# LayerNorm row statistics on ScalarE, the maxima fold on one operand, and a new table of orders

## The chip, the core and the metric

The kernel runs on one core of a Trainium2 chip. The metric is the device time of one execution in microseconds (us). The core's engines are TensorE (PE in the profile, its weight loads PEld), VectorE (DVE), ScalarE (ACT) and GpSimd (POOL); SyncE (SP) issues nearly all DMAs. Each engine works through its own instruction stream strictly in order and waits on semaphores for the others.

## The reference

Four attention layers act on x of 1 x 2048 x 512, in the order A, B, A, B; both kinds have 32 heads of 16 dimensions.

```python
x = x + _A_ref(_layernorm(x), A_wqkv, A_wo)   # 8 keys per query, 2 apart
x = x + _B_ref(_layernorm(x), B_wqkv, B_wo)   # sliding window of 256 keys
x = x + _A_ref(_layernorm(x), A_wqkv, A_wo)
x = x + _B_ref(_layernorm(x), B_wqkv, B_wo)

def _layernorm(x, axis=-1, eps=1e-5):
    m = jnp.mean(x, axis=axis, keepdims=True)
    v = jnp.var(x, axis=axis, keepdims=True)
    return (x - m) / jnp.sqrt(v + eps)
```

## The kernel before

The 2048 rows are cut into 8 chunks of 256 rows (`C`), and a layer works chunk by chunk; layers 0 and 2 are of kind A, 1 and 3 of kind B. In names such as `xn0_5_1` the digits are the layer, the chunk and the half (128 rows) of the chunk.

**Norm.** `norm(l, c)` handles one chunk: for each half, VectorE's `bn_stats` and `bn_aggr` (L750, L751) give mean and variance in `mv`; GpSimd turns them into scale and shift in `rs` (`rstd`, L754 to L757); ScalarE writes the normalised rows `xn` (L769) and their 16-bit rounding `xm` (L781); GpSimd or VectorE writes the remainder over `xn` (L772); and four transposing DMAs on SyncE's queue bring both into `xh` and `xl` (L775, L778). `xn` has two buffers, one for each half, so a chunk's `xn` may be written only when the remainder of the norm before has left by DMA.

**Layer A.** Projections `pq` (L802 to L804; three 16-bit matmuls for each product), copied to `q` and `kv` by ScalarE; products `pr` of query and shifted keys and their sums (L960, L967, on VectorE or GpSimd); a reduction on TensorE into `L`; the softmax over 8 keys in `e`; spread on TensorE (`pb`), weighted values `pw` (L1046) and their sums `o`.

**Layer B.** `eh` and `el` (16-bit parts of the projections) go through DRAM (`re`) into the stacked operands `stk`. TensorE forms scores twice. The first time (`st`, `sf`, L1130) is for the maximum over each query's keys: VectorE masks (L1153) and reduces them (L1154, L1173) into the tile `m`, which holds for each row one maximum from `st` and one from `sf`. `mturn` takes the larger of the two (L1183) and transposes the result (L1184); ScalarE and GpSimd split it into two 16-bit parts `mt` (L1187 to L1191), and it goes through DRAM (`md`) into spare rows of `stk`. The second time (`sk_F`, `sk_L`, `sk_H`, L1224) the matmul thereby subtracts the maximum; ScalarE takes the exponential `p` (L1234), GpSimd masks it (L1245), TensorE multiplies with the values (`av`, L1259).

Both kinds end in `finish`: `oh` and `ol`, output projection `po` (L823), and `done` (L869), in which VectorE adds `po` to the rows of x in `xr`. The norm of layer B works on those rows.

**The order.** Every step is a task with an engine, a duration, and what it reads and writes. The table `ORDER` gives each task its place in its engine's stream; a negative number puts the task on its other engine (`alt`: VectorE in place of GpSimd or the reverse). `Plan.order()` plays the streams against the durations, which sets only in what sequence the engines' instructions are written out and which buffer a tile gets; within an engine the table decides. In the scope `W`, 80 groups of three matmuls on constants (`idle`) fill TensorE while the weights are prepared.

Of the kernel before, what the change touches and what calls it, by code (L numbers as in the profile page):

```python
# [1415 lines left out]
```

## Time and profile before

| | |
|---|---|
| time, median of 3 runs | 1371.41 us (1362.38 to 1377.51) |
| the profiled execution's own time | 1373.37 us |
| its span, first to last instruction | 1371.6 us |
| mean granted TensorE clock | 0.973 |
| PE busy | 1246.9 us, 91% of the span |
| DVE busy | 1142.3 us, 83% |
| POOL busy | 955.4 us, 70% |
| ACT busy | 733.7 us, 53% |
| DMA | 140.17 MB, mean 102 GB/s |

The busy time of an engine is that of its instructions; an engine that waits for another is idle. A row of groups gives the source line, the engine, the operation, its tiles (written <- read), the count, the busy time, the mean of one, and the idle time before these instructions with what ended it. A row of waits reads "engine, instruction <- what it waited for: us in total, times, longest".

### The profile page before, as it was taken

To read this page: it belongs to the slowest core of one execution; us is meant where nothing else is said; L and a number is where in the kernel's file an instruction comes from. 1 tells how busy PE (TensorE), PEld (TensorE's weight loads), DVE (VectorE), ACT (ScalarE), POOL (GpSimd) and SP (SyncE) were. 2 spreads that over 40 slices of the span, in tenths; PEclk is the share of its full clock that TensorE was granted. 3 is DMA by queue.
4 is the path that set the end of the run, shared out by engine and by line. 5 is a ranking of instruction groups with operands and counts; after the bars stand their busy time and mean duration, and the time that the engine had idled before them with its cause. 6 is when DMAs were issued, how large, how long until landed. Compare 5 with 4: busy or idle time off the path is not lost.

```text
span 1371.6 us, 47863 instructions
## 1 busy us (share of the span) xinstructions
PE 1246.9 (91%) x20752; PEld 847.8 (62%) x20752; DVE 1142.3 (83%) x1482; ACT 733.7 (53%) x1035; POOL 955.4 (70%) x1013
## 2 busy tenths in 40 slices
PE   6869999989998898999999999998998999998877
PEld 4546666657566665666667666766666666664544
DVE  5968978887887888789899999798987988988574
ACT  7543454646555464655556464555555566365544
POOL 4357678778686877877686768888678877666233
PEclk9989999999999999999999999999999999999989
DMA  8204243334434332444434444433444434234322
GB/s 279 60 16 137 60 126 90 121 84 121 82 78 129 94 112 69 115 110 106 119 90 124 106 115 108 99 108 78 136 100 111 93 97 118 54 96 112 97 73 64
DMA packets 172467, 140.17 MB, mean 102 GB/s; under 512 B 105184, under 2 KB 131296, under 8 KB 172256
## 3 DMA queue, kind: packets, MB, share of 16 engines
q1 hardware_dynamic: 172000, 136.85, 38.1%
q8 instruction: 162, 2.65, 0.8%
q14 instruction: 49, 0.40, 0.1%
q10 hardware_dynamic: 256, 0.26, 0.1%
HBM read 67.11 MB, written 43.48 MB: 81 GB/s over the span
## 4 chain that ended last, share of the span: by engine, by line
PE 20%; DVE 12%; DMA 7%; SPq 4%; issue 3%; ACT 2%; POOL 2%; ACTq 0%; DVEq 0%; POOLq 0%
PE av L1259 3%; PE po L823 3%; PE pq L802 3%; PE pq L803 2%; PE pq L804 2%; DVE st L1153 2%; DVE m L1154 2%; DVE pw L1046 2%; DVE m L1173 2%; PE st L1130 2%; DMA xl<-xn 1%; DMA stk<-re 1%; SPq L1098 1%; DMA os<-scr 1%; SPq L1314 1%
## 5 line engine op out<-in xcount | busy, mean ns | idle before, releaser
L960 POOL TENSOR_TENSOR pr<-kv,q 128x1024 f32<-128x1024 f32 x76 | 170.5, 2253 | 41.9 <-DVE pr L967 16.2
L1153 DVE COPY_PREDICATED st<-maskt,st 128x512 f32<-128x512 int16 x224 | 154.0, 687 | 50.1 <-PE st L1130 46.1
L1234 ACT ACTIVATE p_H<-sk_H,scales 128x1024 f32<-128x1024 f32 x128 | 142.4, 1113 | 93.8 <-PE sk_H L1224 82.3
L1234 ACT ACTIVATE p_F<-sk_F,scales 128x1024 f32<-128x1024 f32 (+1 forms) x128 | 135.6, 1060 | 102.8 <-PE sk_F L1224 97.5
L1245 POOL TENSOR_SCALAR_AFFINE_SELECT p_H<-p_H 128x1024 f32<-128x1024 f32 x128 | 143.0, 1118 | 50.5 <-ACT p_H L1234 50.2
L1245 POOL TENSOR_SCALAR_AFFINE_SELECT p_L<-p_L 128x1024 f32<-128x1024 f32 x112 | 125.7, 1125 | 59.6 <-ACT p_L L1234 59.3
L1046 DVE TENSOR_TENSOR pw<-pb,kv 128x1024 f32<-128x1024 f32 x128 | 151.0, 1211 | 17.6 <-PE pb L1033 16.1
L1173 DVE TENSOR_REDUCE m<-sf 128x8 f32<-128x1024 f32 x120 | 144.8, 1211 | 22.8 <-PE sf L1130 22.5
L1154 DVE TENSOR_REDUCE m<-st 128x4 f32<-128x512 f32 x224 | 154.7, 691 | 7.7
L1234 ACT ACTIVATE p_L<-sk_L,scales 128x1024 f32<-128x1024 f32 x112 | 124.0, 1113 | 67.1 <-PE sk_L L1224 64.2
L1130 PEld LDWEIGHTS <-stk 48*128 48x128 f16 x2880 | 90.3, 95 | 109.3 <-issue 69.6
L1224 PEld LDWEIGHTS <-stk 64*128 64x128 f16 x2880 | 90.8, 95 | 100.8 <-issue 60.1
L1053 POOL TENSOR_TENSOR pw<-pw 128x512 f32<-128x512 f32 x87 | 110.9, 1274 | 28.8 <-DVE pw L1046 27.7
L1130 PE MATMUL st<-stk,stk 48*128 48x128 f16 x1920 | 97.4, 220 | 22.9 <-DMA stk<-re 8.0
L967 POOL TENSOR_TENSOR pr<-pr,pr 128x1024 f32<-128x1024 f32 x31 | 73.0, 2356 | 26.0 <-DVE pr L960 25.6
L1259 PE MATMUL av<-p_H,v 128*32 128x128 f32 x2048 | 81.1, 276 | 0.8 <-POOL p_H L1245 0.8
L1051 DVE TENSOR_REDUCE o<-pw 128x128 f32<-128x1024 f32 x41 | 79.9, 1953 | 0.2
L1259 PE MATMUL av<-p_F,v 128*32 128x128 f32 x1920 | 78.9, 280 | 0.7 <-ACT p_F L1234 0.6
L803 PE MATMUL pq<-xl,wA1h 128*128 128x256 f16 x256 | 70.7, 276 | 6.6 <-DMA xl<-xn 6.6
L960 DVE TENSOR_TENSOR pr<-kv,q 128x1024 f32<-128x1024 f32 x52 | 72.6, 1411 | 4.7 <-POOL pr L967 4.0
L803 PE MATMUL pq<-xl,wB1h 128*128 128x256 f16 x256 | 70.5, 275 | 6.5 <-DMA xl<-xn 6.3
L823 PEld LDWEIGHTS <-oh 128*32 128x32 f16 x2048 | 49.2, 98 | 43.5 <-issue 5.6
(194 smaller groups left out, 3592.7 us busy)
## 6 DMA issues: line engine op xcount, KB each, us to landing
stk<-re SPq DMA_DIRECT2D x256, 96.0 KB
re<-eh SPq DMA_DIRECT2D x128, 128.0 KB
xm<-xr SPq DMA_DIRECT2D x32, 256.0 KB
re<-el SPq DMA_DIRECT2D x64, 128.0 KB
xr<-xm SPq DMA_DIRECT2D x16, 512.0 KB
oc<-os SPq DMA_DIRECT2D x120, 64.0 KB
os<-scr SPq DMA_DIRECT2D x15, 512.0 KB
x<-in_A_x_dram SPq DMA_DIRECT2D x8, 512.0 KB
```

Source lines behind the costliest of these rows:

```text
L803: nc.tensor.matmul(ps[mp].t[:, i], wh, xl, start=False, stop=False)
L960: E.tensor_mul(pr.t, window(kv[1].t, m, P * n, P), qb)
L1046: nc.vector.tensor_mul(pw.t, pb.t.unsqueeze(1).broadcast_to([P, 2, W, 64]), v)
L1053: E.tensor_add(t[:, :, 0:4], t[:, :, 0:4], t[:, :, 4:8])
L1130: nc.tensor.matmul(ps.t[:, par, at * P : (at + 1) * P], stk[hf, 0][r, col, qb * P : (qb + 1) * P], stk[hf, kt][r, col, kb * P : (kb + 1) * ...
L1153: nc.vector.copy_predicated(v[:, :, 0::2], maskt[:, 0:P].bitcast(I16).unsqueeze(1).unsqueeze(1).broadcast_to([P, 2, 2, P]), v[:, :, 1::2])
L1154: nc.vector.tensor_reduce(out=m[:, 0, :, us[0]], in_=v[:, :, 0::2], op=ALU.max, axis=AX.X)
L1173: nc.vector.tensor_reduce(out=o, in_=v, op=ALU.max, axis=AX.X)
L1224: nc.tensor.matmul(ps.t[:, par, at * P : (at + 1) * P], stk[hf, kt][r, col, kb * P : (kb + 1) * P], stk[hf, 0][r, col, qb * P : (qb + 1) * ...
L1234: nc.scalar.activation(o, i, AF.Exp, scale=scl["B", 1])
L1245: nc.gpsimd.affine_select(out=v, in_=v, pattern=[[0, 8], [-1 if kind == "L" else 1, P]], compare_op=ALU.is_gt if kind == "L" else ALU.is_g ...
L1259: nc.tensor.matmul(acc.t[32 * mm : 32 * mm + 32, hq, qb * P : (qb + 1) * P], v[:, 17 * (H * kb + h) : 17 * (H * kb + h) + 32], p[:, mm % 2 ...
```

## The change

1. **Row statistics.** `bn_stats` and `bn_aggr` leave VectorE. In an A norm ScalarE sums each row while it copies it (`rowsum`), and then sums the squares of (sum - 512 x) (`rowvar`); both write a full-size output into `xn` that nobody reads. In a B norm the sum comes from `done`, whose VectorE instruction gets an accumulator output; ScalarE makes only `rowvar`. `rstd` keeps its four GpSimd instructions, with other constants.
2. **One-operand maxima.** `mturn` no longer takes the larger of two operands with `tensor_tensor`; one `tensor_reduce` reads `m` alone, twice by a broadcast, and writes 32 columns into `mr`; the transpose writes to `mt`, from which ScalarE reads. In the first chunk of a layer a copy of 16 columns comes first.
3. **Orders.** All of `ORDER` is replaced, found with durations for VectorE, ScalarE, GpSimd and SyncE that lie somewhat above the trace's; the durations written in the plan, and `TURN`, change a little as well. TensorE keeps the same instructions in equal numbers.

```diff
-TURN = 0.15
+TURN = 0.17
...
-        def stats(t):
-            nc.vector.bn_stats(b6[t].t, xb.t[:, t])
-            nc.vector.bn_aggr(mv.t[:, t], b6[t].t)
+        xns = [buf("pxn", [P, D], F32, "xn", f"xn{l}_{c}_{t}") for t in range(2)]
+        vxq = [Val(x) for x in xns]
+
+        def rowsum(t):
+            nc.scalar.activation(xns[t].t, xb.t[:, t], AF.Copy, accum_out=mv.t[:, 0, t : t + 1])
+
+        def rowvar(t):
+            nc.scalar.activation(xns[t].t, xb.t[:, t], AF.Square, bias=mv.t[:, 0, t : t + 1], scale=-float(D), accum_out=mv.t[:, 1, t : t + 1])
...
-            plan.add("DVE", 0.82, lambda t=t: stats(t), r=[vx[t]], w=[vmv[t], Val(b6[t])])
-        plan.add("POOL", 2.3, rstd, r=vmv, w=[vrs])
+            if sums:
+                plan.add("ACT", 0.72, lambda f=rowsum, t=t: f(t), r=[vx[t]], w=[vsm[t], vxq[t]])
+            plan.add("ACT", 0.72, lambda f=rowvar, t=t: f(t), r=[vx[t], vsm[t]], w=[vsq[t], vxq[t]])
+        plan.add("POOL", 1.95, rstd, r=vsq, w=[vrs])
...
-                nc.vector.scalar_tensor_tensor(xt, ps.t, scl[T, 3], xt, op0=ALU.mult, op1=ALU.add)
+                kw = {"accum_out": mv.t[:, 0, t : t + 1]} if mv else {}
+                nc.vector.scalar_tensor_tensor(xt, ps.t, scl[T, 3], xt, op0=ALU.mult, op1=ALU.add, **kw)
...
-                a, b = (m[:, z, :, :, 1] if first else m[:, z].rearrange("p a u q -> p (a u q)") for z in range(2))
-                nc.vector.tensor_tensor(out=a, in0=a, in1=b, op=ALU.max)
-                nc.vector.transpose(mr.t, m.rearrange("p z a u q -> p (z a u q)"))
+                v = m.rearrange("p z a u q -> p (a u q) z")
+                o = mr.t.rearrange("p (r g) -> p r g", r=2)
+                if first:
+                    nc.vector.tensor_copy(o[:, :, 0::2], v[:, 0::2, 0].unsqueeze(1).broadcast_to([P, 2, 8]))
+                    o, v = o[:, :, 1::2], v[:, 1::2]
+                nc.vector.tensor_reduce(out=o, in_=v.unsqueeze(1).broadcast_to([P, 2, *v.shape[1:]]), op=ALU.max, axis=AX.X)
+                nc.vector.transpose(mt.t.bitcast(F32).rearrange("p a b -> p (a b)"), mr.t)
```

Counted over the whole streams, the new table also moves tasks from GpSimd to VectorE: VectorE now does 61 of the 128 products of L960 (52 before), 38 of the 64 sums of L967 (33 before) and 21 of the 30 multiplications of L1337 (9 before).

Three places show how instructions moved. Line numbers of the new kernel are up to 22 higher. The first is VectorE's stream in layer 3, chunk 3, where the maxima of the third of four head groups (`mr3_3_2`) are folded. Before:

```order
L960 TENSOR_TENSOR pr2_5_0_1_0_19181<-kv2_5_1_18023,q2_5_18631 128x1024
L1173 TENSOR_REDUCE m0_118<-sf3_3_2_1_19204 128x2x4
L1183 TENSOR_TENSOR m0_118<-m0_118 128x16
L1184 STREAM_TRANSPOSE mr3_3_2_19238<-m0_118 128x32
L1077 SCALAR_TENSOR_TENSOR el3_4_1_19263<-pq3_4_1_1_19165,eh3_4_1_19240 128x2x256
L1153 COPY_PREDICATED st3_3_3_3_19254<-maskt_133,st3_3_3_3_19254 128x4x128
```

Now:

```order
L1191 TENSOR_REDUCE m0_118<-sf3_3_2_1_19074 128x2x4
L1171 COPY_PREDICATED st3_3_2_3_19104<-maskt_133,st3_3_2_3_19104 128x4x128
L1172 TENSOR_REDUCE m0_118<-st3_3_2_3_19104 128x2x2
L1205 TENSOR_REDUCE mr3_3_2_19143<-m0_118 128x32
L1206 STREAM_TRANSPOSE mt3_3_2_19145<-mr3_3_2_19143 128x32
L887 SCALAR_TENSOR_TENSOR xr3_2_18874<-po3_2_1_18920,scales1_160,xr3_2_18874 128x512
```

The fold reads one operand, and the `done` of another chunk (L887, L869 before) now stands directly behind it, where `el` stood.

The second is ScalarE's stream between two norms in layers 0 and 1: that of layer 1, chunk 3 ends and that of layer 0, chunk 5 begins. Before:

```order
L769 ACTIVATE xn1_3_0_4961<-xr0_3_3753,rs1_3_4903 128x512
L769 ACTIVATE xn1_3_1_4971<-xr0_3_3753,rs1_3_4903 128x512
L781 CAST xm1_3_0_4980<-xn1_3_0_4961 128x512
L781 CAST xm1_3_1_4992<-xn1_3_1_4971 128x512
L938 ACTIVATE kv0_4_1_4107<-pq0_4_1_1_4599 128x2x256
L1234 ACTIVATE p1_2_2_H_5023<-sk1_2_2_H_5006,scales1_160 128x1024
L861 CAST oh1_1_4951<-oc1_1_4650 128x4x128
L938 ACTIVATE kv0_4_2_5060<-pq0_4_2_0_4908 128x2x256
L769 ACTIVATE xn0_5_0_5114<-x0_5_4538,rs0_5_4827 128x512
```

Now:

```order
L783 ACTIVATE xn1_3_0_4876<-xr0_3_4404,rs1_3_4889 128x512
L954 COPY q0_4_4698<-pq0_4_0_1_4869 128x512
L795 CAST xm1_3_0_4974<-xn1_3_0_4876 128x512
L878 CAST oh1_1_4934<-oc1_1_4429 128x4x128
L956 ACTIVATE kv0_4_1_3966<-pq0_4_1_1_4547 128x2x256
L760 ACTIVATE xn0_5_0_5069,mv0_5_5070<-x0_5_4976 128x512
L956 ACTIVATE kv0_4_2_5081<-pq0_4_2_0_4909 128x2x256
L1256 ACTIVATE p1_2_2_H_5097<-sk1_2_2_H_5032,scales1_160 128x1024
L760 ACTIVATE xn0_5_1_5113,mv0_5_5070<-x0_5_4976 128x512
L1256 ACTIVATE p1_2_3_L_5142<-sk1_2_3_L_5124,scales1_160 128x1024
L763 ACTIVATE xn0_5_1_5113,mv0_5_5070<-x0_5_4976,mv0_5_5070 128x512
L763 ACTIVATE xn0_5_0_5069,mv0_5_5070<-x0_5_4976,mv0_5_5070 128x512
```

The first instruction that writes the next norm's `xn` is now a row sum (L760); two instructions stand between it and the last rounding of the norm before, where four stood, and the exponential `p1_2_2_H` is behind it instead of ahead. The normalising writes of this norm (L783) follow 8 and 14 rows behind the last one shown.

The third is ScalarE's stream at the very start, from its first instruction on. Before:

```order
L663 ACTIVATE wA1l_164,amA1_200<-stk1_1_116 128x1024
L663 ACTIVATE wA1l_164,amA1_200<-stk0_1_113 128x1024
L769 ACTIVATE xn0_0_1_211<-x0_0_177,rs0_0_202 128x512
L769 ACTIVATE xn0_0_0_219<-x0_0_177,rs0_0_202 128x512
L663 ACTIVATE wA0l_162,amA0_225<-stk0_0_112 128x1024
L781 CAST xm0_0_1_232<-xn0_0_1_211 128x512
L663 ACTIVATE wA0l_162,amA0_225<-stk1_0_115 128x1024
L714 ACTIVATE wA1h_163<-stk0_1_113,scales0_159 128x1024
```

Now:

```order
L760 ACTIVATE xn0_0_1_191,mv0_0_192<-x0_0_179 128x512
L760 ACTIVATE xn0_0_0_194,mv0_0_192<-x0_0_179 128x512
L763 ACTIVATE xn0_0_0_194,mv0_0_192<-x0_0_179,mv0_0_192 128x512
L763 ACTIVATE xn0_0_1_191,mv0_0_192<-x0_0_179,mv0_0_192 128x512
L665 ACTIVATE wA1l_164,amA1_198<-stk1_1_116 128x1024
L665 ACTIVATE wA1l_164,amA1_198<-stk0_1_113 128x1024
L783 ACTIVATE xn0_0_1_191<-x0_0_179,rs0_0_200 128x512
L795 CAST xm0_0_1_211<-xn0_0_1_191 128x512
L783 ACTIVATE xn0_0_0_194<-x0_0_179,rs0_0_200 128x512
L665 ACTIVATE wA0l_162,amA0_220<-stk0_0_112 128x1024
L795 CAST xm0_0_0_235<-xn0_0_0_194 128x512
L665 ACTIVATE wA0l_162,amA0_220<-stk1_0_115 128x1024
```

Four statistics instructions stand ahead of the first squares over the weights (`wA1l`, which give the weights' scale), and behind the last row shown a square over `wA2l` comes before `wA1h`, the first scaled weights, which the first projection needs.

More of the change, by code (lines that the diff above doesn't have):

```diff
@@ L733 @@
     x_in = {}
+    x_sum = {}
     x_mid = {}
@@ L740, in norm @@
         xb, vx = x_in[c]
-        mv = buf("psm", [P, 2, 2], F32, "mv", f"mv{l}_{c}")
+        sums = layers[l] == "A"
+        if sums:
+            mv = buf("psm", [P, 2, 2], F32, "mv", f"mv{l}_{c}")
+            vsm = [Val(mv), Val(mv)]
+        else:
+            mv, vsm = x_sum[c]
         rs = buf("psm", [P, 2, 2], F32, "rs", f"rs{l}_{c}")
-        b6 = [buf("ps1", [P, 6], F32, "b6", f"b6{l}_{c}_{t}") for t in range(2)]
-        vmv, vrs = [Val(mv), Val(mv)], Val(rs)
+        vsq, vrs = [Val(mv), Val(mv)], Val(rs)
         xh, xl = (buf("pxt", [P, 4, C], F16, n, f"{n}{l}_{c}") for n in ("xh", "xl"))
@@ L747, in norm @@
         d["vxt"] = []
-        def stats(t):
-            nc.vector.bn_stats(b6[t].t, xb.t[:, t])
-            nc.vector.bn_aggr(mv.t[:, t], b6[t].t)
+        xns = [buf("pxn", [P, D], F32, "xn", f"xn{l}_{c}_{t}") for t in range(2)]
[4 more added lines that the diff above has]
+            nc.scalar.activation(xns[t].t, xb.t[:, t], AF.Square, bias=mv.t[:, 0, t : t + 1], scale=-float(D), accum_out=mv.t[:, 1, t : t + 1])
         def rstd():
-            nc.gpsimd.tensor_scalar(rs.t[:, 0], mv.t[:, :, 1], 1.0e-5, 1.0 / (XS * XS), op0=ALU.add, op1=ALU.mult)
+            nc.gpsimd.tensor_scalar(rs.t[:, 0], mv.t[:, 1], 1.0 / (float(D) ** 3 * XS * XS), 1.0e-5 / (XS * XS), op0=ALU.mult, op1=ALU.add)
             nc.gpsimd.tensor_tensor(out=rs.t[:, 0], in0=rs.t[:, 0], in1=mhalf, op=ALU.pow)
             for t in range(2):
-                nc.gpsimd.tensor_scalar(rs.t[:, 1, t : t + 1], mv.t[:, t, 0:1], rs.t[:, 0, t : t + 1], -1.0, op0=ALU.mult, op1=ALU.mult)
+                nc.gpsimd.tensor_scalar(rs.t[:, 1, t : t + 1], mv.t[:, 0, t : t + 1], rs.t[:, 0, t : t + 1], -1.0 / D, op0=ALU.mult, op1=ALU.mult)
         for t in range(2):
-            plan.add("DVE", 0.82, lambda t=t: stats(t), r=[vx[t]], w=[vmv[t], Val(b6[t])])
-        plan.add("POOL", 2.3, rstd, r=vmv, w=[vrs])
+            if sums:
+                plan.add("ACT", 0.72, lambda f=rowsum, t=t: f(t), r=[vx[t]], w=[vsm[t], vxq[t]])
+            plan.add("ACT", 0.72, lambda f=rowvar, t=t: f(t), r=[vx[t], vsm[t]], w=[vsq[t], vxq[t]])
+        plan.add("POOL", 1.95, rstd, r=vsq, w=[vrs])
         for t in range(2):
-            xn = buf("pxn", [P, D], F32, "xn", f"xn{l}_{c}_{t}")
+            xn = xns[t]
             hi = buf("pxm", [P, D], F16, "xm", f"xm{l}_{c}_{t}")
-            vxn, vhi, vlo, vh, vl = Val(xn), Val(hi), Val(xn), Val(xh), Val(xl)
+            vxn, vhi, vlo, vh, vl = vxq[t], Val(hi), Val(xn), Val(xh), Val(xl)
             d["vxt"] += [vh, vl]
@@ L846, in finish @@
         x_in[c] = xb, vx
+        if T == "A":
+            mv = buf("ps1", [P, 2, 2], F32, "mvB", f"mv{l}_{c}")
+            x_sum[c] = mv, [Val(mv), Val(mv)]
         oh, ol = (buf("poh", [P, 4, C], F16, "o", f"o{z}{l}_{c}") for z in "hl")
@@ L865, in finish, with done @@
             proj_n(T, 3, oh, ol, parts or [vh, vl], t, ps, vps)
-            def done(t=t, ps=ps):
+            def done(t=t, ps=ps, mv=x_sum[c][0] if T == "A" else None):
                 xt = xb.t[:, t]
-                nc.vector.scalar_tensor_tensor(xt, ps.t, scl[T, 3], xt, op0=ALU.mult, op1=ALU.add)
-            plan.add("DVE", 0.67, done, r=[vps, vscl[T, 3], vx[t]], w=[vx[t]])
+                kw = {"accum_out": mv.t[:, 0, t : t + 1]} if mv else {}
+                nc.vector.scalar_tensor_tensor(xt, ps.t, scl[T, 3], xt, op0=ALU.mult, op1=ALU.add, **kw)
+            plan.add("DVE", 0.78, done, r=[vps, vscl[T, 3], vx[t]], w=[vx[t], *([x_sum[c][1][t]] if T == "A" else [])])
             if T == "A":
@@ L928, in first @@
                     nc.gpsimd.tensor_copy(kv[s].t[:, :, :HALO], halo[l, c - 1, s][0].t)
-            plan.add("POOL", 0.5, first, r=[] if c == 0 else [halo[l, c - 1, s][1]], w=[vhalo[s]])
+            plan.add("POOL", 0.32, first, r=[] if c == 0 else [halo[l, c - 1, s][1]], w=[vhalo[s]])
         for s in range(3):
@@ L944, in layer_a @@
                 halo[l, c, s] = ha, vha
-                plan.add("POOL", 0.45, lambda s=s, ha=ha: nc.gpsimd.tensor_copy(ha.t, kv[s].t[:, :, C:]), r=vkv[s], w=[vha])
+                plan.add("POOL", 0.26, lambda s=s, ha=ha: nc.gpsimd.tensor_copy(ha.t, kv[s].t[:, :, C:]), r=vkv[s], w=[vha])
         L = buf("q_pj", [P, W, 64], F32, "pj", f"L{l}_{c}")
@@ L991, in clip @@
                                         compare_op=ALU.is_ge, fill=NEG, base=-HALO, channel_multiplier=0)
-            plan.add("POOL", 4.0, clip, r=[ve0], w=[ve1])
+            plan.add("POOL", 0.95, clip, r=[ve0], w=[ve1])
             src_, vsrc = e, ve1
@@ L1057, in layer_a @@
                 plan.add("DVE", 1.13, weigh, r=[vpb[th], *vkv[2], vhalo[2]], w=[vpw])
-                plan.add("POOL", 2.7, total, r=[vpw], w=[vr], alt=("DVE", 1.84))
+                plan.add("POOL", 2.58, total, r=[vpw], w=[vr], alt=("DVE", 1.84))
         finish(l, c, o, vo)
@@ L1179, in layer_b, with mturn @@
             vmr, vmt, vmd = Val(mr), [Val(mt), Val(mt)], Val(md)
-            def mturn(m=m, mr=mr):
-                a, b = (m[:, z, :, :, 1] if first else m[:, z].rearrange("p a u q -> p (a u q)") for z in range(2))
-                nc.vector.tensor_tensor(out=a, in0=a, in1=b, op=ALU.max)
-                nc.vector.transpose(mr.t, m.rearrange("p z a u q -> p (z a u q)"))
+            def mturn(m=m, mr=mr, mt=mt):
+                v = m.rearrange("p z a u q -> p (a u q) z")
[5 more added lines that the diff above has]
+                nc.vector.transpose(mt.t.bitcast(F32).rearrange("p a b -> p (a b)"), mr.t)
             def mhigh(mr=mr, mt=mt):
-                nc.scalar.activation(mr.t, mr.t, AF.Copy, scale=1.0 / MC)
+                nc.scalar.activation(mr.t, mt.t.bitcast(F32).rearrange("p a b -> p (a b)"), AF.Copy, scale=1.0 / MC)
                 nc.scalar.copy(mt.t[:, 0], mr.t)
@@ L1191, in mlow @@
                 nc.gpsimd.tensor_tensor(out=mt.t[:, 1], in0=mr.t, in1=mt.t[:, 0], op=ALU.subtract)
-            plan.add("DVE", 0.65, mturn, r=[vm], w=[vmr])
-            vms = Val(mr)
-            plan.add("ACT", 0.4, mhigh, r=[vmr], w=[vms, vmt[0]])
-            plan.add("POOL", 0.45, mlow, r=[vms, vmt[0]], w=[vmt[1]])
-            plan.add("SP", 0.59, lambda md=md, mt=mt: nc.sync.dma_start(md.t, mt.t), r=vmt, w=[vmd], size=30)
+            plan.add("DVE", 0.33, mturn, r=[vm], w=[vmr, vmt[0]])
+            vms, vml = Val(mr), Val(mt)
+            plan.add("ACT", 0.4, mhigh, r=[vmr], w=[vms, vmt[1]])
+            plan.add("POOL", 0.28, mlow, r=[vms, vmt[1]], w=[vml])
+            plan.add("SP", 0.59, lambda md=md, mt=mt: nc.sync.dma_start(md.t, mt.t), r=[vml], w=[vmd], size=30)
             for z in range(2):
```

10 lines of the change are left out of this document (5 added, 5 removed), and 460 rows, old and new, of the table ORDER.

## The prediction

> **What bounds the kernel now.** I read the busy times of the page first, then the same in three stages, then what TensorE waited for, then the chain of work that ended last.
>
> ```profile
> PE 1246.9 (91%) x20752; PEld 847.8 (62%) x20752; DVE 1142.3 (83%) x1482; ACT 733.7 (53%) x1035; POOL 955.4 (70%) x1013
> 0.00:137.20 137.20, 106.18 (x876) 71.36 (x876) 101.44 (x154) 68.14 (x101) 69.27 (x98) 0.93 0.41 123
> 137.20:1200.20 1063.00, 997.68 (x17124) 688.02 (x17125) 925.52 (x1168) 574.58 (x820) 808.45 (x832) 0.99 0.40 102
> 1200.20:1371.60 171.40, 143.01 (x2755) 88.43 (x2752) 115.36 (x162) 91.01 (x115) 77.66 (x84) 0.91 0.32 89
> ```
>
> The columns of the stages are length, then busy time of PE, PEld, DVE, ACT, POOL, then the granted clock. TensorE is idle for 31.0 us in the start, 65.3 us in the long middle and 28.4 us in the end, 124.7 us together. The change gives it no matmul less, so 1246.9 us stay, and all there is to win is in those 124.7 us. In the middle VectorE, with 925.5 of 1063 us, is the next most loaded.
>
> ```profile
> PE pq L803 <- DMA xl<-xn: 12.9, 14, 2.8
> PE sk_H L1224 <- DMA stk<-md: 7.2, 4, 2.9
> PE st L1130 <- DMA stk<-re: 6.4, 13, 1.1
> PE sk_H L1224 <- DVE m L1154: 3.4, 4, 1.4
> ...
> PE sk_L L1224 <- DVE m L1173: 0.6, 2, 0.3
> ```
>
> These are TensorE's waits in the middle. No wait is long. DMA ends about half of them (the three rows shown, 26.5 us). Between the two rows on `m` stand eight more of their kind (waits on L1154 or L1173), and the ten make 17.1 us: TensorE stands before a score buffer that VectorE has yet to reduce.
>
> ```profile
> PE 20%; DVE 12%; DMA 7%; SPq 4%; issue 3%; ACT 2%; POOL 2%; ACTq 0%; DVEq 0%; POOLq 0%
> 685.90 0.64 DVE m L1183
> ...
> 1328.54 0.99 DVE m L1183
> ```
>
> The first row is the chain's share by engine. The shares add up to half the span, because the chain is traced back only to the middle of the span; so of the latter half TensorE has two fifths and VectorE a quarter. The pieces under it are the first and the last of eleven in which the fold of the maxima is on that chain; the eleven make 7.2 us. **So TensorE is close to its own work, and a quarter of what delays it further is VectorE's stream. ScalarE and GpSimd are hardly on the chain.**
>
> **The maxima.** What does the fold cost?
>
> ```profile
> L1183 DVE TENSOR_TENSOR m<-m 128x16 f32<-128x16 f32 x56 | 31.1, 555 | 1.3
> L1184 DVE STREAM_TRANSPOSE mr<-m 128x32 f32<-128x32 f32 x64 | 13.5, 211 | 2.6
> L1154 DVE TENSOR_REDUCE m<-st 128x4 f32<-128x512 f32 x224 | 154.7, 691 | 7.7
> 1037.78 2.18 POOL L960 TENSOR_TENSOR pr<-kv,q 128x1024 f32<-128x1024 f32 x1
> 1038.27 1.73 DVE L1183 TENSOR_TENSOR m<-m 128x16 f32<-128x16 f32 x1
> 1282.86 0.17 DVE L1183 TENSOR_TENSOR m<-m 128x16 f32<-128x16 f32 x1
> ```
>
> Sixteen columns take 0.555 us in the mean, but 0.17 us at 1282.86 and 1.73 us at 1038.27. In the second case GpSimd's product runs from 1037.78 to 1039.96, and the fold ends at 1040.00: it stood still until GpSimd was through. So 56 x (0.555 - 0.17) = 21.6 us of the 31.1 are standing still. The new reduce is not in the trace; I bound it by 0.17 us (the unhindered fold) and 0.69 us (L1154, which reads eight times as many elements), and take 0.2, since it reads 64 elements. On the chain's latter half the eleven pieces go from 7.2 to 2.2 us, a gain of 5; as the first half has the same work, 10 us in all. If the reduce too waited for GpSimd, this would be 0.
>
> The Trainium skill, "SBUF — State Buffer", section "Who interferes with whom", states that a VectorE instruction with two SBUF inputs contends with a GpSimd one that reads SBUF, and that `tensor_reduce` never does on trn2. The pair at 1038 agrees with the first half; for a reduce out of SBUF no row here shows the second half, and by it the 10 us above would stand.
>
> **The statistics.** The removed pieces and the nearest rows for the new ones:
>
> ```profile
> L750 DVE BATCH_NORM_STATS2 b<-x 128x6 f32<-128x512 f32 x32 | 21.8, 681 | 5.6 <-DMA x<-in_A_x_dram 4.5 <-DMA x<-xd 0.8
> L750 DVE BATCH_NORM_STATS2 b<-xr 128x6 f32<-128x512 f32 x32 | 22.1, 692 | 0.9
> L751 DVE BATCH_NORM_AGGREGATE mv<-b 128x2 f32<-128x6 f32 x64 | 11.7, 182 | 2.2
> L769 ACT ACTIVATE xn<-x,rs 128x512 f32<-128x512 f32 x32 | 25.5, 811 | 19.3 <-POOL rs L757 12.0 <-DMA xl<-xn 7.2
> L781 ACT CAST xm<-xn 128x512 f16<-128x512 f32 x64 | 39.0, 614 | 0.7
> L663 ACT ACTIVATION_READ_ACCUMULATOR wB3l<-stageB 128x1 f32 x2 | 0.4, 190 | 0.0
> 712.20 0.70 DVE b L750
> ...
> 1179.51 0.70 DVE b L750
> ```
>
> VectorE loses 21.8 + 22.1 + 11.7 = 55.6 us. Nine of these pieces lie on the chain between the two rows quoted last. Four of the nine, by their times, belong to A norms (`x`): with about 0.8 us each, 3.2 us leave the chain. Five belong to B norms (`xr`), which are waited for directly, and there ScalarE's square replaces 0.69 + 0.18: 0.81 us (like L769, which also takes a pointer operand) and 0.19 us for the accumulator, so 0.13 us more, 0.6 us for five. `done` gains an accumulator output 32 times. No row shows that on VectorE; I bound it by 0 and by the 0.19 of ScalarE's accumulator, and take 0.15 for the five or so such pieces on the chain, 0.8 us. Net 3.2 - 0.6 - 0.8 = 1.8 us in the traced half, 4 us in all.
>
> A rule speaks against this part: the Trainium skill, "VectorE: DVE Perf Modes", section "Two Vector instructions with no wait between them", counts an operation that also writes out its accumulator as two instructions. ScalarE's separate accumulator rows show that form there; no row shows it on VectorE. By the rule and 0.19 us, the 32 would cost VectorE 6 us of busy time.
>
> **What ScalarE pays.** It gets 32 sums at 0.61 to 0.81 us (L781, L769), 64 squares at 0.81 and 96 accumulator reads at 0.19: 20 to 26, 52 and 18, about 92 us, to 826 us or 60%. It waits for TensorE far more than TensorE for it, so most of that lies in idle time. Two places are not covered. At the start:
>
> ```profile
> 4.54 0.69 DVE L750 BATCH_NORM_STATS2 b<-x 128x6 f32<-128x512 f32 x1 [4.54 <-DMA x<-in_A_x_dram]
> 13.35 1.15 ACT L714 ACTIVATE wA1h<-stk,scales 128x1024 f16<-128x1024 f32 x1 [0.24 <-DVE scales L689]
> ```
>
> x is there at 4.54 us. By the durations above and 1.15 us for 1024 columns, four statistics instructions take 3.6 to 4.0 us, two squares over `wA1l` 2.3, and the seven rows behind them (two normalising writes, two roundings, three squares) 6.3; so `wA1h` starts at about 17 us instead of 13.35, or a little earlier, since neighbouring rows overlap slightly. How much of these 3.5 us reaches the end of the start depends on what else holds the first projection: 0 to 3.5; I take 3, near the upper end, because the scaled weights stand directly ahead of it. The second place is behind each norm:
>
> ```profile
> 317.62 0.59 ACT L938 ACTIVATE kv<-pq 128x512 f32<-128x512 f32 x1
> 320.17 0.81 ACT L769 ACTIVATE xn<-x,rs 128x512 f32<-128x512 f32 x1 [1.96 <-DMA xl<-xn]
> 321.71 1.12 ACT L1234 ACTIVATE p_L<-sk_L,scales 128x1024 f32<-128x1024 f32 x1 [0.25 <-PE sk_L L1224]
> ```
>
> ScalarE waits 1.96 us for a buffer of `xn` whose remainder the transposing DMA still reads, with the exponentials queued behind it. But the exponential behind it still waits 0.25 us for TensorE: up to 2.2 us of such a wait are free here. In the new order the row sum comes earlier by 1.5 us of ScalarE's work at this place (an exponential and a copy fewer ahead of it), so the wait there is about 3.5 us. I take 2 us for all such places, as most will find TensorE's two score buffers filled ahead.
>
> **The load moved and the new order.** VectorE takes over 9 products, 5 sums and 12 multiplications from GpSimd. Their prices on VectorE, and TensorE's waits on `m` in the end:
>
> ```profile
> L960 DVE TENSOR_TENSOR pr<-kv,q 128x1024 f32<-128x1024 f32 x52 | 72.6, 1411 | 4.7 <-POOL pr L967 4.0 <-ACT q L936 0.6
> L967 DVE TENSOR_TENSOR pr<-pr,pr 128x1024 f32<-128x1024 f32 x33 | 42.7, 1296 | 1.3 <-POOL pr L960 0.9
> L1337 DVE TENSOR_TENSOR oc<-oc,os 128x512 f32<-128x512 f32 x9 | 7.1, 789 | 6.4 <-DMA os<-scr 3.5 <-DMA xm<-xr 2.0 <-issue 0.7
> PE st L1130 <- DVE m L1173: 2.3, 4, 1.3
> ...
> PE sf L1130 <- DVE m L1173: 0.5, 1, 0.5
> ```
>
> That adds 12.7 + 6.5 + 9.5 = 29 us to VectorE, less about 4 us for what goes back elsewhere. So VectorE stands at 1142 - 56 - 20 + 5 + 25 = 1096 us, its idle time grows from 229 to some 270 us, and the waits of TensorE on `m` shrink in about that proportion: of 17.1 us in the middle and 10.2 in the end (eight rows, the first and last shown), 27 x (1 - 229/270) = 4 us, beyond what the chain's own pieces give. What the new places bring by themselves no row can show. It lies between a loss as large as the gains above and half of the middle's 65 us. One thing is visible: an A norm's normalising writes now stand far behind its statistics, so part of the 12.0 us in the row of L769 above, in which ScalarE is held by `rs` with the exponentials behind it, goes away. I take 2 us.
>
> **The sum**, against the profiled execution's own 1373.4 us: -10 (maxima) -4 (statistics on the chain) -4 (VectorE's load) -2 (places) +3 (start) +2 (ScalarE) = -15, so 1358. The median of the three runs lies 2 us below the profiled execution: **1356 us**, 1.1% faster. With the bounds (reduce at 0.69 us or stopped, start without loss, no accumulator cost) this reaches from 1342 to 1366.
>
> **The rivals.**
> *Nothing to see.* The pieces leave VectorE, but TensorE then waits for the DMA of `stk` and `xl` a little later at the same place, as half the middle's waits end there already. For it: no wait of TensorE on VectorE is above 1.4 us. Then about a third of the 20 us comes through and the 5 us of loss remain: 1371 - 7 + 5 = 1369; with a reduce that stands still as the old fold did, the same. 1362 to 1378.
> *ScalarE holds the exponentials: slower.* An A norm's first row sum waits for the DMA that empties `xn`. What the earlier norm still has to do from its rounding to the landing:
>
> ```profile
> L778 SPq DMA_TRANSPOSE xl<-xn x64: 1188/1244/2348, 13.5 to 1262.8; - x64
> L772 POOL TENSOR_TENSOR xn<-xn,xm x44: 1152/1162/1598, 12.1 to 1258.0; 128x512 f16<-128x512 f32 x44
> 756.64 3.98 DMA xl<-xn
> ```
>
> Remainder (1.16 us), issue (1.24) and transfer (3.98, a piece of the chain) make 6.4 us. The wait decides from 2.2 us on; in 14 of the 15 A norms that follow one of B it could be up to 5 us, so 14 x 2.8 = 39 us late against 15 won: 1371 + 39 - 15 = 1395, or 1385 to 1406. Against it: the four waits in the old trace make 7.2 us, though the distances there are of the same kind.
> *Far more.* If the new places free half of the middle's idle time, 33 us, plus the 5 of net gain in start and end: 1371 - 38 = 1333, or 1320 to 1342.
>
> **How the numbers follow.** Forecast 0.50 (1342 to 1362), nothing to see 0.22, slower 0.14, far more 0.14. A measurement of this kernel tells about 1% from no change, so faster is below 1357.7: 0.14 and 0.38 of the forecast's 0.50 make 0.52; within 1%, 0.12 + 0.22 = 0.34; slower 0.14. The range 1330 to 1385 holds the forecast, the case of nothing to see and most of the case of far more below it.
>
> **What would show it.** The fold's row as a reduce of about 0.2 us with little spread: right; at 0.5: wrong. VectorE's busy time near 1096, ScalarE's near 826, GpSimd's clearly under 955. TensorE's idle time in the middle near 52 us. `wA1h` at 16 us or later. A row "ACT xn <- DMA xl<-xn" well over 30 us, with TensorE waiting for `p`, would speak for the slower rival. The prediction is wrong if the new order changes the start or the end by more than 10 us, which no term above contains.

## The result, and the profile after

| | before | after |
|---|---|---|
| time, median | 1368.64 us (1362.38 to 1377.51, 4 runs) | 1345.87 us (1344.20 to 1350.18, 4 runs) |
| ratio | | 0.9871, 95% interval 0.9831 to 0.9911 |
| profiled execution | 1373.37 us | 1344.20 us |
| span / mean granted clock | 1371.6 us / 0.973 | 1342.5 us / 0.986 |

In a second series (6 runs of after, 26 of before) it was 1347.15 against 1366.82 us, ratio 0.9856 (0.9815 to 0.9896). The change makes the kernel 1.3 to 1.4% faster, about 20 us. The forecast was 1356 us in a range of 1330 to 1385.

The busy times of the changed kernel on its page, then in three stages (start, middle, the last 171.4 us; the columns as before):

```profile
PE 1232.4 (92%) x20752; PEld 844.7 (63%) x20752; DVE 1097.3 (82%) x1416; ACT 798.6 (59%) x1227; POOL 918.1 (68%) x993
```
```profile
0.00:137.20 137.20, 108.17 (x897) 73.22 (x898) 99.10 (x140) 78.49 (x129) 66.96 (x97) 0.94 0.41 117
137.20:1171.10 1033.90, 980.95 (x17002) 679.70 (x17000) 878.84 (x1108) 623.72 (x974) 764.75 (x807) 0.99 0.42 105
1171.10:1342.50 171.40, 143.33 (x2858) 91.84 (x2856) 119.37 (x170) 96.35 (x126) 86.38 (x91) 0.98 0.34 91
```

TensorE is idle for 29.0, 52.9 and 28.1 us in the stages, 110.1 together; before it was 124.7. Those 14.6 us are half of the 29.1 us between the two spans. **The other half is TensorE's busy time: the same 20752 matmuls take 1232.4 instead of 1246.9 us.** VectorE is 45 us less busy, GpSimd 37 us less, ScalarE 65 us more.

TensorE's waits over the whole span, "what waited <- what for: us in total, times, longest":

```profile
PE pq L817 <- DMA xl<-xn: 9.6, 10, 2.2
PE st L1148 <- DMA stk<-re: 6.2, 11, 1.3
...
PE sk_L L1246 <- DMA stk<-md: 4.5, 4, 1.6
PE sk_L L1246 <- DVE m L1172: 4.3, 6, 2.0
...
PE sf L1148 <- DVE m L1172: 3.8, 9, 0.8
```

All waits on DMAs together fall from 37.9 to 27.2 us; those on VectorE's `m` stay (27.9 before, 25.8 now, eleven rows, of which two are shown), although VectorE does less.

The new instructions:

```profile
L763 ACT ACTIVATE xn<-xr,mv 128x512 f32<-128x512 f32 x32 | 22.8, 715 | 15.1 <-DVE xr L887 15.1
L760 ACT ACTIVATE xn<-x 128x512 f32<-128x512 f32 x32 | 20.1, 627 | 25.4 <-DMA xl<-xn 13.7 <-DMA x<-in_A_x_dram 9.6 <-DMA x<-xd 1.4
...
L1205 DVE TENSOR_REDUCE mr<-m 128x32 f32<-128x64 f32 x56 | 12.2, 218 | 1.4
...
L1203 DVE COPY mr<-m 128x16 f32<-128x16 f32 x8 | 4.2, 523 | 0.1
...
L887 DVE DVE_READ_ACCUMULATOR xr<-po,scales,xr 128x1 f32 x32 | 2.6, 82 | 0.0
```

The reduce takes 0.218 us where the two-operand fold took 0.555.

### The profile page after: what moved, and what is told of

It is laid out like the page before. It is cut to its first block, busy times and chain, and to the rows that moved or that the text cites. A ratio compares the mean times of both kernels' runs of the same rounds, so it can differ in the third digit from the quotient of the medians.

```text
span 1342.5 us, 48022 instructions
## 1 busy us (share of the span) xinstructions
PE 1232.4 (92%) x20752; PEld 844.7 (63%) x20752; DVE 1097.3 (82%) x1416; ACT 798.6 (59%) x1227; POOL 918.1 (68%) x993
## 4 chain that ended last, share of the span: by engine, by line
PE 43%; DVE 17%; DMA 14%; ACT 9%; SPq 6%; POOL 6%; issue 6%; ACTq 0%; DVEq 0%; POOLq 0%
PE pq L816 7%; PE pq L817 6%; PE pq L818 6%; PE po L837 6%; PE av L1281 6%; DVE pw L1064 3%; DMA xl<-xn 3%; DVE st L1171 3%; DMA stk<-re 3%; PE st L1148 3%; DVE m L1172 2%; DVE m L1191 2%; SPq L1336 2%; DMA os<-scr 2%; DMA xh<-xm 1%
## 5 line engine op out<-in xcount | busy, mean ns | idle before, releaser
L978 POOL TENSOR_TENSOR pr<-kv,q 128x1024 f32<-128x1024 f32 x67 | 149.3, 2236 | 13.5 <-DVE pr L985 6.5
L1064 DVE TENSOR_TENSOR pw<-pb,kv 128x1024 f32<-128x1024 f32 x128 | 151.1, 1213 | 3.8 <-PE pb L1051 3.2
L1071 POOL TENSOR_TENSOR pw<-pw 128x512 f32<-128x512 f32 x88 | 112.1, 1274 | 20.1 <-DVE pw L1064 20.0
L978 DVE TENSOR_TENSOR pr<-kv,q 128x1024 f32<-128x1024 f32 x61 | 83.7, 1389 | 1.9 <-POOL pr L985 1.0
L985 POOL TENSOR_TENSOR pr<-pr,pr 128x1024 f32<-128x1024 f32 x26 | 61.4, 2362 | 30.1 <-DVE pr L978 29.8
L816 PE MATMUL pq<-xh,wA1h 128*128 128x256 f16 x256 | 72.3, 283 | 3.7 <-DMA xh<-xm 3.4
L816 PE MATMUL pq<-xh,wA0h 128*128 128x256 f16 x256 | 71.1, 278 | 5.0 <-ACT kv L956 4.1
```

The source lines that it names most:

```text
L816: nc.tensor.matmul(ps[mp].t[:, i], wh, xh, start=k == 0, stop=False)
L978: E.tensor_mul(pr.t, window(kv[1].t, m, P * n, P), qb)
L1064: nc.vector.tensor_mul(pw.t, pb.t.unsqueeze(1).broadcast_to([P, 2, W, 64]), v)
L1071: E.tensor_add(t[:, :, 0:4], t[:, :, 0:4], t[:, :, 4:8])
```

## The experiments

Differences to the changed kernel are taken from the two ratios to the kernel before, times 1366.8 us, since the runs lie on several chips; each ratio is to runs of the kernel before on the same chip (medians of 1364.8 to 1369.4 us). By the intervals of the ratios, such a difference is uncertain by 6 to 8 us either way, and one to the kernel before by 4 to 5 us. "Idle" is TensorE's, span less busy time; "on m" and "on DMA" are its waits. These and VectorE's busy time belong to one profiled execution; for the old B statistics that was the slowest of twelve (1368.66 us), for the short statistics the fastest (1356.90 us).

| kernel | median us (runs) | ratio to before (95%) | DVE busy | idle | on m | on DMA |
|---|---|---|---|---|---|---|
| before | 1366.82 (26) | 1 | 1142.3 | 124.7 | 27.9 | 37.9 |
| after, again | 1347.15 (6) | 0.9856 (0.9815 to 0.9896) | 1098.9 | 112.1 | 26.2 | 25.8 |
| old fold | 1356.35 (11) | 0.9924 (0.9898 to 0.9950) | 1113.4 | 118.9 | 29.2 | 24.6 |
| old statistics | 1365.27 (12) | 0.9989 (0.9962 to 1.0015) | 1146.8 | 130.9 | 41.0 | 29.4 |
| new order alone | 1377.38 (10) | 1.0069 (1.0041 to 1.0096) | 1162.5 | 132.8 | 43.5 | 25.6 |
| old B statistics | 1360.71 (12) | 0.9966 (0.9939 to 0.9992) | 1120.0 | 131.0 | 40.3 | 26.3 |
| unread statistics added | 1368.10 (12) | 1.0013 (0.9987 to 1.0039) | 1147.3 | 131.7 | 40.1 | 20.3 |
| before, statistics twice | 1382.74 (6) | 1.0131 (1.0098 to 1.0164) | 1180.3 | 133.8 | 37.2 | 33.8 |
| before, fold twice | 1380.20 (6) | 1.0110 (1.0081 to 1.0140) | 1176.6 | 141.3 | 37.7 | 41.9 |
| before, B statistics new | 1366.07 (12) | 1.0002 (0.9977 to 1.0028) | 1113.8 | 126.1 | 22.0 | 43.5 |
| after, statistics into xm | 1349.98 (6) | 0.9886 (0.9849 to 0.9924) | 1096.3 | 113.4 | 24.8 | 26.7 |
| after, 26 back on GpSimd | 1356.96 (12) | 0.9925 (0.9901 to 0.9949) | 1081.4 | 123.5 | 24.8 | 32.9 |
| before, short statistics | 1362.63 (12) | 0.9962 (0.9934 to 0.9990) | 1111.4 | 117.5 | 19.0 | 41.7 |

### The four combinations inside the new order

The changed kernel again, without an edit:

> The changed kernel once more, beside the three below on the same chip. If the granted clock follows the kernel (the steadier feeding of TensorE in the new order), all executions lie at 0.98 or above and TensorE is busy for about 1232 us again (1344 to 1350 us in all). If the clock of the first profiled execution was chance, executions near 0.973 turn up, with about 1247 us busy and a time near 1358 us. The kernel before should show the opposite: never above 0.976 by the first theory, up to 0.986 by the second.

The clock came out at 0.983 to 0.988 in all ten executions of the changed kernel in the two series, and at 0.971 to 0.985 (median 0.977) in the 26 of before. So it goes with the kernel, but not as sharply as the first theory had it: 15 of the 26 executions of before lie above its limit of 0.976, and the ranges touch.

The old fold:

```diff
-                nc.vector.tensor_reduce(out=o, in_=v.unsqueeze(1).broadcast_to([P, 2, *v.shape[1:]]), op=ALU.max, axis=AX.X)
-                nc.vector.transpose(mt.t.bitcast(F32).rearrange("p a b -> p (a b)"), mr.t)
...
+                nc.vector.tensor_tensor(out=a, in0=a, in1=b, op=ALU.max)
+                nc.vector.transpose(mt.t.bitcast(F32).rearrange("p a b -> p (a b)"), m.rearrange("p z a u q -> p (z a u q)"))
```

> The changed kernel with the old fold alone: two operands, in place on the tile m, 0.56 us in the mean instead of 0.22. By the terms of the prediction the fold is worth 10 us, so about 1356 us, with TensorE's waits on m longer by some 5 to 8 us. By the rival that the table of orders brings nearly everything, under 3 us more than the changed kernel (up to 1349 us), as VectorE's additional 20 us fall into its idle time.

The old statistics; A norms' pieces stand in VectorE's stream where the row sums stood in time, B norms' directly behind `done`:

```diff
-                plan.add("ACT", 0.72, lambda f=rowsum, t=t: f(t), r=[vx[t]], w=[vsm[t], vxq[t]])
-            plan.add("ACT", 0.72, lambda f=rowvar, t=t: f(t), r=[vx[t], vsm[t]], w=[vsq[t], vxq[t]])
...
+            plan.add("DVE", 0.82, lambda t=t: stats(t), r=[vx[t]], w=[vsq[t], Val(b6[t])], place=p)
```

> The changed kernel with the row statistics back on VectorE (0.69 and 0.18 us for each half of a chunk) and done without its accumulator. By the terms of the prediction the statistics are worth 4 us on the chain, less 3 at the start and 2 of ScalarE's waits: between 1344 and 1351 us, with the first scaled weights starting about 2 us earlier. By the rival that VectorE's load decides, 47 us more on VectorE cost a fifth to a half of that: 1355 to 1368 us. By the rival that the row sums in xn hold ScalarE, this kernel is faster than the changed one by 3 to 10 us.

Both edits together leave the order alone:

> The new table of orders with the old fold and the statistics on VectorE: of the change only the order is left, and VectorE carries what it took over from GpSimd without the relief. By the terms of the prediction (2 us for new places, VectorE busier by 25 us) between 1366 and 1376 us, no faster than the kernel before. By the rival that the order alone brings the gain, 1345 to 1356 us, with a granted clock of 0.98 or above.

The old fold costs 9.3 us, as the terms had it, though the waits on `m` grow by only 3 us (26.2 to 29.2) where 5 to 8 were expected. The old statistics cost 18 us, not 4. The order alone is 10.6 us slower than the kernel before by the medians (9.4 by the ratio), at the far end of what the terms allowed. The fold's row in the run with the old fold, then TensorE's waits with the order alone:

```profile
L1201 DVE TENSOR_TENSOR m<-m 128x16 f32<-128x16 f32 x56 | 34.9, 622 | 1.3
```
```profile
PE st L1145 <- DVE m L1169: 7.6, 11, 1.3
PE sk_H L1239 <- DVE m L1169: 7.0, 8, 2.5
...
PE sf L1145 <- DVE m L1188: 6.2, 3, 3.2
```

These are three of twelve rows on `m`, 43.5 us in all: the new table takes 12 us off TensorE's waits on DMAs (37.9 to 25.6) and puts 16 us onto those on VectorE. The fold and the statistics then take these off again. Such a result could also mean only that the table doesn't suit the old pieces; the next runs bear on that.

### Is it VectorE's time, or the norm's chain?

`load` runs `bn_stats` and `bn_aggr` into a tile that nobody reads:

```diff
+            plan.add("DVE", 0.82, lambda t=t: load(t), r=[vx[t]], place=p)
```

> The changed kernel with the old statistics run on VectorE besides, into a tile that nobody reads, at the places that they had in the run with the old statistics; ScalarE, GpSimd and all waits stay as in the changed kernel. It adds 56 us to VectorE and nothing to any norm's own chain. If the statistics' 18 us came from VectorE's time, this costs as much or a little more: 1364 to 1369 us, with TensorE's waits on m near 40 us. If they came from the norm's chain (sum, square, scale, normalise), it costs under 6 us: up to 1353 us.

```profile
PE st L1163 <- DVE m L1187: 9.6, 10, 3.0
...
PE sf L1163 <- DVE m L1206: 5.1, 3, 3.1
```

It costs 21 us, with 40.1 us on `m`. No task of a norm reads these instructions' result, so the 18 us of the old statistics are in the main VectorE's time (48 us more busy in both runs) and not a slower norm. A B norm isn't wholly untouched, though: the unread statistics of the first half stand between the two halves of `done`, so the second half ends some 0.9 us later, and ScalarE's squares wait 21.3 us for `done` instead of 16.6.

Only the B norms' half on VectorE:

```diff
+            else:
+                plan.add("DVE", 0.82, lambda t=t: stats(t), r=[vx[t]], w=[vsq[t], Val(b6[t])], place=at_done[c][t].place + 0.5)
```

> The changed kernel with only the B norms' statistics back on VectorE (32 times 0.69 and 0.18 us directly behind done, which loses its accumulator); the A norms' stay on ScalarE. By the terms of the prediction the B half of the change loses 1.4 us in the traced half, 2.8 us in all, so this kernel should be 3 us faster than the changed one, about 1344 us. By the theory that VectorE's time itself is the price (18 us for the 48 us that all statistics bring back), 25 us more on VectorE cost 9 us: about 1356 us.

It costs 15 us instead of bringing 3; the sign of that term was wrong. With an uncertainty of 6.5 us this also allows the 9 us of the other theory. ScalarE's normalising write now waits for `rs` three times as long. The row of the changed kernel (second series), then of this one:

```profile
L783 ACT ACTIVATE xn<-xr,rs 128x512 f32<-128x512 f32 x32 | 25.8, 810 | 7.8 <-POOL rs L769 7.7
```
```profile
L795 ACT ACTIVATE xn<-xr,rs 128x512 f32<-128x512 f32 x32 | 25.8, 810 | 23.2 <-POOL rs L778 23.1
```

This is no additional wait. In the changed kernel the square ahead of that write waits 16.6 us for `done`, and here there is no such square: 16.6 + 7.8 = 24.4 us against 23.2. ScalarE waits as long as before, at another instruction.

### What VectorE's time costs in the old order

Adding to it, the statistics and the fold each twice:

```diff
             nc.vector.bn_aggr(mv.t[:, t], b6[t].t)
+            nc.vector.bn_stats(unread[:, 0:6], xb.t[:, t])
+            nc.vector.bn_aggr(unread[:, 6:8], unread[:, 0:6])
```
```diff
                 nc.vector.tensor_tensor(out=a, in0=a, in1=b, op=ALU.max)
+                nc.vector.tensor_tensor(out=a, in0=a, in1=b, op=ALU.max)
```

> The kernel before, in its old order, with every statistic computed a second time on VectorE directly behind the first, into a tile that nobody reads: 56 us more on VectorE, which was the cost that the change takes away. By the prediction's price (about 8 us for the statistics and the load together, out of 56) 1373 to 1377 us. If VectorE's time has the same price in the old order as in the new one (a third of it), 1383 to 1387 us. If the old order had room on VectorE and only the new one lacks it, under 3 us: up to 1370 us.

> The kernel before with the two-operand maximum of the fold run twice in place, which adds 64 instructions of about 0.5 us (33 us) to VectorE at the place where the fold stands. By the prediction's price (10 us for 21.6 us of standing still) 1379 to 1383 us. If the fold is priced like other time of VectorE (a third), 1376 to 1379 us. If TensorE's waits on the DMAs cover it, under 4 us more.

The first adds 54 us of instructions and costs 18.0 us by the medians, a third. The second adds the row of L1184, 35.5 us, and costs 15.4 us, more than two fifths. Whether a fold is really dearer, since it stands directly ahead of what TensorE waits for, these runs don't tell: VectorE's busy time rises by 38.0 us in the first and 34.3 in the second, as other instructions get shorter, and by that the two prices are alike, at 0.47 and 0.45.

```profile
L1184 DVE TENSOR_TENSOR m<-m 128x16 f32<-128x16 f32 x56 | 35.5, 635 | 1.9
L1183 DVE TENSOR_TENSOR m<-m 128x16 f32<-128x16 f32 x56 | 29.1, 520 | 1.3
```

Taking from it, with nothing added elsewhere:

```diff
-            nc.vector.bn_stats(b6[t].t, xb.t[:, t])
+            nc.vector.bn_stats(b6[t].t, xb.t[:, t, 0:64])
```

> The kernel before with bn_stats over 64 of the 512 columns: the statistics are computed from an eighth of each row, all else is as before. It takes about 35 us off VectorE in the old order, at the places where the change takes them away, and adds nothing to any engine. If VectorE's time has one price, a third, in both directions, 11 us are won: 1353 to 1356 us. If the old order turns the time won into waits for the DMAs, as with the B norms' statistics in the old order, under 4 us: 1362 us or more, with TensorE's waits on m at 22 us or less and those on DMAs above 40 us.

```profile
L750 DVE BATCH_NORM_STATS2 b<-xr 128x6 f32<-128x64 f32 x32 | 7.2, 226 | 0.9
L750 DVE BATCH_NORM_STATS2 b<-x 128x6 f32<-128x64 f32 x32 | 6.9, 215 | 6.4 <-DMA x<-in_A_x_dram 5.4 <-DMA x<-xd 0.9
```

`bn_stats` takes 14.1 instead of 43.9 us; that brings 5.2 us by the ratio (1.4 to 9.0), 6.8 by the medians: about a fifth of the time removed, between the two expectations. The waits on `m` fall to 19.0 us, those on DMAs rise to 41.7.

Moving the B norms' half to ScalarE in the old order, with squares where `done` ends:

```diff
-            plan.add("DVE", 0.82, lambda t=t: stats(t), r=[vx[t]], w=[vmv[t], Val(b6[t])])
...
+                plan.add("ACT", 0.9, lambda f=rowvar, t=t: f(t), r=[vx[t], vsm[t]], w=[vsq[t], vxq[t]], place=at[t])
```

> The kernel before, in its old order and with its old fold, with only the B norms' statistics as the change makes them: the sum from an accumulator of done, the square on ScalarE, put into ScalarE's old stream where done ends. It takes 28 us off VectorE and gives 3 back. If VectorE's time has one price, a third, in both orders, 8 us less than the kernel before: 1355 to 1359 us. If that part only pays in the new order, 1362 us or more. By the terms of the prediction 3 us more than before: about 1368 us.

```profile
PE pq L827 <- DMA xl<-xn: 18.1, 14, 3.2
PE st L1158 <- DMA stk<-re: 10.4, 14, 2.0
```

Nothing comes through (0.0%, from 0.2% faster to 0.3% slower), with VectorE 28 us less busy and the waits on `m` at 22.0. The waits on DMAs stand at 43.5 us: what the prediction's rival of "nothing to see" described, but in the old order. I placed the squares by hand, so a better place isn't excluded. ScalarE also pays here: its waits for `done` and `rs` in the norms make 37.0 us, against 31.4 for `rs` in the kernel before.

### ScalarE's waits, and the load on GpSimd

```diff
-            nc.scalar.activation(xns[t].t, xb.t[:, t], AF.Copy, accum_out=mv.t[:, 0, t : t + 1])
+            nc.scalar.activation(xms[t].t.bitcast(BF16), xb.t[:, t], AF.Copy, accum_out=mv.t[:, 0, t : t + 1])
```

> The changed kernel with the unread output of the row sums and squares going into the tiles xm in place of xn; xm comes free when the rounding has left, some 4 us earlier than the remainder in xn. ScalarE's 14 us of waits for the transposing DMA in front of a row sum should fall to under 5 us. If such waits hold up the exponentials behind them, as the slower rival of the prediction has it, 3 to 8 us are won: 1339 to 1344 us. If TensorE's filled score buffers cover them, it stays within 2 us of the changed kernel (1345 to 1349 us).

ScalarE's wait ahead of the row sums:

```profile
ACT xm L762 <- DMA xh<-xm: 9.7, 5, 3.6
```

The waits only went from 13.7 to 9.7 us, as `xm` is held too, and the time didn't fall (4 us more, uncertain by 8). This is too small a step to test the rival.

The load: `BACK` holds a place on GpSimd for each of 26 tasks.

```diff
+            at = BACK[back].get(self.seen.get(back, 0))
...
+        if at is not None:
+            t.place = at
+            if eng == "DVE":
+                t.eng, t.us = alt
```

> The changed kernel with 26 of the instructions that the new table took from GpSimd to VectorE put back on GpSimd, into gaps of its stream (11 products of L978, 6 sums of L985, 9 multiplications of L1360): VectorE loses about 30 us, GpSimd gains about 50 us. If VectorE's time is the price wherever it is taken away, a third of it, 8 to 10 us are won: 1337 to 1340 us. If the load was moved because GpSimd's answers came too late, it costs 3 to 12 us: 1350 to 1360 us.

```profile
PE 1233.8 (91%) x20752; PEld 845.3 (62%) x20752; DVE 1081.4 (80%) x1390; ACT 798.6 (59%) x1227; POOL 969.7 (71%) x1019
```

VectorE is only 17 us less busy, GpSimd 50 us more, and it costs 9.4 us. So in the new kernel, which has this time on VectorE, the moved load is no loss; but the places on GpSimd were my own, and better ones may exist. No run beats the changed kernel.

## Why the prediction was right or wrong

**The total** fell into the forecast's own range (1342 to 1362), 10 us below the value. But several of its terms were off and in part they cancelled: statistics and VectorE's load, forecast to bring 8 us, brought 18, and the order, whose new places were forecast to bring 2, alone lost 10.6. That the sum came out within the range is in part luck.

**"1246.9 us stay" was wrong.** This premise, from which the room left to win was taken (124.7 us in all, 65 in the middle), left out the clock, though the rows of the stages showed it at 0.93, 0.99 and 0.91. In the profile before, behind a wait of TensorE, first the instructions, then the windows (us, busy times, the granted clock third from the end):

```profile
359.86 0.28 PE L802 MATMUL pq<-xh,wA1h 128*128 128x256 f16 x1
362.43 0.39 PE L803 MATMUL pq<-xl,wA1h 128*128 128x256 f16 x1 [2.29 <-DMA xl<-xn]
362.62 0.42 PE L804 MATMUL pq<-xh,wA1l 128*128 128x256 f16 x1
```
```profile
358.49:361.90 3.41, 1.65 (x41) 0.92 (x33) 3.31 (x6) 2.19 (x4) 3.07 (x4) 1.00 0.92 72
361.90:365.31 3.41, 2.88 (x19) 1.38 (x20) 0.41 (x2) 0.99 (x1) 0.45 (x1) 0.51 0.72 155
365.31:368.72 3.41, 3.41 (x52) 2.47 (x52) 3.35 (x4) 2.30 (x6) 2.25 (x3) 0.99 0.06 9
```

After 2.29 us of waiting the clock is at half for 3.4 us, and a matmul takes 0.42 instead of 0.28 us. Over windows of 1 us I added up the missing clock: 37.5 us before, 18.8 us after, which is 22 and 11 such stretches. TensorE's busy time within them times the missing share is 32.1 us before and 17.1 after, 22.5 with the old fold, 22.6 with the old statistics, 27.7 with the order alone. The rest of its busy time is 1214.8, 1215.3, 1213.6, 1215.3 and 1215.7 us (1213 to 1219 over all fourteen profiles): the matmuls' own time does stay, and the 14.5 us are stretches at half clock that no longer occur. So a wait that goes can bring its length and a part of 1.7 us more. The median clock is 0.974 to 0.980 in the five kernels with the old order and 0.981 to 0.986 in the eight with the new one, also in those that take 1365 us or more. That the old order's waits lie so that they cost more clock is what this suggests; it isn't shown. Of the profiled difference of 29 us some 9 were chance: the profiled execution of before had a low clock and lay 6.6 us above the median of 26, that of after 2.9 us below its median of 6. By the median clocks, 0.977 and 0.986, the clock missing is 31 and 19 us; with the shares of it that fell into busy time above, TensorE's busy time holds about 10 of the 20 us in a typical pair as well. This is an estimate.

**Maxima, -10: right.** 9.3 us in the new order (uncertain by 6.5), and for the reason given: all 64 reduces take 0.178 to 0.224 us. Of them, 21 run wholly within an instruction of GpSimd of over 1 us, with 0.209 to 0.224 us. In the profile before, each of the 35 folds of over 0.3 us ends within 0.08 us behind an instruction of GpSimd. From the profile after, first a reduce beside a product of GpSimd, then a copy of a first chunk beside one:

```profile
857.90 2.19 POOL L978 TENSOR_TENSOR pr<-kv,q 128x1024 f32<-128x1024 f32 x1
859.55 0.22 DVE L1205 TENSOR_REDUCE mr<-m 128x32 f32<-128x64 f32 x1
...
781.76 2.19 POOL L978 TENSOR_TENSOR pr<-kv,q 128x1024 f32<-128x1024 f32 x1
781.89 2.10 DVE L1203 COPY mr<-m 128x16 f32<-128x16 f32 x1
```

Only the copies in first chunks were overlooked; they take 0.523 us in the mean and stand still like the old fold. The prediction found no row of a reduce out of SBUF. There was one, L1051 over `pw`, whose 41 instances take 1.85 to 2.06 us; their small spread already spoke for this.

**Statistics on the chain, -4, and VectorE's load, -4: mis-sized, and the B half had the wrong sign.** Counting the pieces on one traced chain gave 8 us for 56 us; in the new order it is 18. In the old order the removal of 30 us brought a fifth of it, near the prediction's price. The accumulator of `done` cost 2.6 us of VectorE in all, not 0.15 but 0.08 us each. It is an instruction of its own, as the Trainium skill, "VectorE: DVE Perf Modes", section "Two Vector instructions with no wait between them", has it; its row above agrees.

**New places, -2: the step that failed besides the clock.** The order was costed as a sum of moved pieces, independent of the rest. Alone it loses 10.6 us; with the two reliefs, 30 us come back. In the old order, the half of the statistics that could be tried brought nothing. The new fold and the A norms' new statistics weren't tried in the old order. The runs show what the order does: alone it shortens TensorE's waits on DMAs (37.9 to 25.6 us) and lengthens those on `m` (27.9 to 43.5), and the two reliefs take the latter back to 26.2. So the new order needs the time that they free on VectorE. That the old order could use less of such time is shown for the B half (nothing) and for the short statistics (a fifth); for the whole change it is an estimate.

**Start, +3: too much.** `wA1h` starts at 15.18 us, not 17, and the first `done` hardly moves:

```profile
15.18 2.17 ACT L716 ACTIVATE wA1h<-stk,scales 128x1024 f16<-128x1024 f32 x2
...
93.31 0.75 DVE L887 SCALAR_TENSOR_TENSOR xr<-po,scales,xr 128x512 f32<-128x512 f32 x1 [2.38 <-PE po L837]
```

It started at 92.78 before. Squares of 0.715 us instead of 0.81 account for part of it.

**ScalarE, +2: about nothing.** Row sums wait 13.7 us for `xl` (7.2 before, the old first write), far from the 30 that would have spoken for the slower rival. TensorE's waits on `p` went from 12.3 to some 10 us. ScalarE ended at 798.6 us busy, not 826: sums, squares and accumulator reads make 84 us by their rows, not 92, and the engine's busy time rose by only 65.

**The signs named in advance.** VectorE 1097 (1096 forecast), TensorE's idle time in the middle 52.9 (52), GpSimd 918: met. They would have looked the same had the fold brought all of it; they tested the load, not the reason.

## What to carry to other kernels

Time on an engine that is not the bound has no fixed price: here its worth went from nothing (28 us moved to ScalarE in the old order) over a fifth (30 us taken away there) to a third and more (some 50 us added, in either order). Cost an order and the relief that it was made for together, or run the four combinations. And of an engine whose clock drops behind its waits, the busy time is no constant: look at the granted clock just behind the gaps before calling it a floor.
